# Attention and feed-forward in one kernel: other PSUM pools, one addition and one scaling moved, up to the first feed-forward

## The chip, the cores and the metric

The kernel runs on one core of one Trainium2 chip. The metric is the device time of one execution in microseconds (us). The engines are TensorE (PE, with its weight loads as PEld), VectorE (DVE), ScalarE (ACT), GpSimd (POOL), and SyncE (SP), which here issues every DMA.

## The reference

Inputs are q, k and v for 4 batches, 8 heads, 768 positions and head size 64, and two weights, 512x2048 and 2048x512, all float32 in value (the weights arrive as 64-bit words).

```
scores = q @ k.T / sqrt(64)
keep   = (key < n_sink) | (0 <= query - key < window)      # n_sink 4, window 128
a      = exp(scores - max);  a = a / (sum(a) + 1e-9)       # scores outside keep: -1e9
x      = (a @ v), heads side by side                       # 3072 rows of 512
h      = x @ w_in
g      = h if h >= 1, 0 if h <= -1, else (h + 1)^2 / 4
out    = g @ w_out
```

## The kernel before

The work on attention is cut into 64 units: one head and one half of the sequence (three blocks of 128 queries) of one batch. Eight units, one for each head, make a chunk, and a chunk of 384 finished rows goes through the feed-forward. The first 20 units (`NATIVE`) multiply in plain float32; each such product is a pair of records in the trace. Later units split the operands into two rounded parts. Attention of one chunk is interleaved with the feed-forward of the chunk before. Before the first feed-forward there is no such partner: the first ten units (0 to 9) run against the decoding of six weight blocks alone.

A native unit n goes through these steps:

- **S**: three products of q and k (L240), each into a PSUM bank of the pool `ps_a`. VectorE reads the bank, adds the mask and takes the row's extreme (L244); ScalarE takes the exponential and its sum (L247).
- **The scaling**: 1e-9 is added to the three sums on GpSimd (L252), VectorE takes the reciprocal (L253), and the three blocks of p are multiplied by it, on the engines that `NORM` names: block 0 (128 columns in the first half of a sequence) on VectorE (L267), blocks 1 and 2 (260 columns) on ScalarE (L265).
- **T**: two groups of transposes (L325, L327), each into a bank of `ps_a`, copied out by ScalarE (L328, L332).
- **V**: for two heads together, the product with v (L368) into a bank of `ps_a`, copied into `xn` by ScalarE (L370), then split in two parts by ScalarE and VectorE (L480, L481) as input of the feed-forward.

The feed-forward's first product (L440) writes the pool `ps_h` (2 banks), the second (L459) the pool `ps_o` (3 banks); `ps_a` has 3 banks. So until the first feed-forward five of the eight banks stand empty, and the three of `ps_a` go round among S, T and V. A bank is handed on when its last reader is done.

TensorE runs in the order in which the program is written: for each n, S of unit n, T of unit n-1, and, for odd n, V of units n-3 and n-2. The other engines' order is set by a scheduler with its own estimate of times, and each runs its list strictly in that order. SyncE's list holds, for each unit, the loads of q and k (two buffers: the load for unit n+2 waits for S of unit n), and behind them the loads of weight blocks. A weight block is numbered here w0, w1, ... in the order of use; it is decoded by four VectorE instructions (L151, L152, L153, L155) and a ScalarE cast (L154). Small tiles `vs_r` (44x64) for units after the 20th are loaded and cast early too (L296, L298).

Of the kernel before, what the change touches and what calls it, by code (L numbers as in the profile page):

```python
# [8 lines left out]
F32 = mybir.dt.float32  # L9
# [4 lines left out]
ALU = mybir.AluOpType  # L14

B, H, S, D = 4, 8, 768, 64
DM, DFF = 512, 2048
P = 128
NT = S // P
CT = 3  # L20
# [6 lines left out]
NATIVE = 20  # L27
# [1 line left out]

KL_POOL = range(20, 24)  # L30
GL_POOL = 0
NORM = "vaa"

CHECK = range(34, 34 + 2 * NJ)

# [15 lines left out]
def attn_ffn(ctx, tc, qk, vx, vs, par, w_in, w_out, out):  # L51
    nc = tc.nc
# [5 lines left out]
    ps_a = ctx.enter_context(tc.tile_pool(name="ps_a", bufs=3, space=bass.MemoryType.PSUM))  # L58
    ps_h = ctx.enter_context(tc.tile_pool(name="ps_h", bufs=2, space=bass.MemoryType.PSUM))
    ps_o = ctx.enter_context(tc.tile_pool(name="ps_o", bufs=3, space=bass.MemoryType.PSUM))  # L60
# [168 lines left out]
    def scores(u, i):  # L229
        b, h, t0 = u  # L230
        qs, k_s = st["qk", u]
        if i == 0:
            st["p", u] = [att.tile([P, CT, 260], F32, name="p"), att.tile([P, 2 * CT], F32, name="stat")]
        p, stat = st["p", u]
        t = t0 + i
        lo = KB if t == 0 else 0
        c0 = i * KB if t0 else max(0, (i - 1) * KB)
        ps = ps_a.tile([P, 512], F32, name="ps_a")
        for j, q in enumerate(qs):
            nc.tensor.matmul(ps[:, lo:260], lhsT=q[:, i * P:(i + 1) * P], rhs=k_s[:, c0:c0 + 260 - lo],  # L240
                             start=(j == 0), stop=(j == len(qs) - 1))
        peak_i = peak[:, units.index(u), i:i + 1]
        m = (m0, m1n if units.index(u) < NATIVE else m1, m2)[min(t, 2)]
        nc.vector.tensor_tensor_reduce(  # L244
            out=p[:, i, lo:260], in0=ps[:, lo:260], in1=m, scale=-0.0625 if units.index(u) < NATIVE else -0.125, scalar=3.0e38,
            op0=ALU.add, op1=ALU.min, accum_out=peak_i)
        nc.scalar.activation(p[:, i, lo:260], p[:, i, lo:260], AF.Exp, bias=peak_i, scale=-1.0,  # L247
                             accum_out=stat[:, i:i + 1])
        if i < CT - 1:
            return  # L250
        st.pop(("qk", u))
        nc.gpsimd.tensor_scalar(stat[:, CT:2 * CT], stat[:, 0:CT], 1.0e-9, None, op0=ALU.add)  # L252
        nc.vector.reciprocal(stat[:, CT:2 * CT], stat[:, CT:2 * CT])  # L253
        i0 = int(t0 == 0)
        c0 = 0
        if units.index(u) >= NATIVE:

            c0 = P
            nc.vector.tensor_tensor(p[:, i0:, KB:260], p[:, i0:, KB:260], p[:, i0:, 0:P], op=ALU.add)  # L259
        for i in range(CT):  # L260
            lo = KB if t0 + i == 0 else c0
            r = stat[:, CT + i:CT + i + 1]
            eng = NORM[i] if units.index(u) < NATIVE else "v"
            if eng == "a":
                nc.scalar.activation(p[:, i, lo:260], p[:, i, lo:260], AF.Copy, scale=r)  # L265
            else:
                (nc.gpsimd if eng == "p" else nc.vector).tensor_scalar(p[:, i, lo:260], p[:, i, lo:260], r, None,  # L267
                                                                       op0=ALU.mult)
        if units.index(u) < NATIVE:
            sk = None  # L270
        else:
            sk = att.tile([P, CT * NSINK], F32, name="sk")[:, :(CT - i0) * NSINK]
            nc.vector.tensor_copy(sk.rearrange("p (i s) -> p i s", s=NSINK), p[:, i0:, P:KB])
        st["p", u] = (p, sk)
# [78 lines left out]
    def av2(u):  # L353

        b, h, t0 = u
        T = CT * P
        pt = st.pop(("pt", u)).bitcast(F32).rearrange("p a i c q -> p a (i c q)")
        v_s = st.pop(("v", b, h // 2))
        st.pop(("sp", u))
        ps = ps_a.tile([P, 512], F32, name="ps_a")  # L360

        terms = [(2, 2 * CT - 1, 2 * CT)] + [(i, 2 * i + 1, 2 * i + 3) for i in range(CT - 1)] + [None]
        for n, t in enumerate(terms):
            for a in range(2):
                k, s0, s1 = t or (CT, 2 * CT - 1, 2 * CT)
                rhs = pt[:, a, s0 * P:s1 * P] if t else spn[(h + a) % 4]
                c = s0 // 2 * P
                nc.tensor.matmul(ps[a * D:a * D + D, c:c + (s1 - s0) * P], lhsT=v_s[:, k, a], rhs=rhs,  # L368
                                 start=(n == 0), stop=(n == len(terms) - 1))
        nc.scalar.copy(xn[:, h // 2, :], ps[:, :T])  # L370
# [41 lines left out]
    units = [(b, h, t0) for b, t0 in chunks for h in range(H)]  # L412

    def attn_steps(n):
        us = {k: units[n - k] for k in (-1, 0, 1, 2) if 0 <= n - k < len(units)}
        steps = []
        if n == 0:
            steps.append((0.0, lambda: load(us[0])))
        if -1 in us:
            steps.append((0.0, lambda: load(us[-1])))  # L420
        if 1 in us:
            steps.append((0.0, lambda: values(us[1])))
        qk = [(0.43 if n < NATIVE else 0.22, lambda i=i: scores(us[0], i)) for i in range(CT) if 0 in us]
        tp = [(0.43, lambda i=i: transp(us[1], i)) for i in range(2 if n - 1 < NATIVE else 1) if 1 in us]
        pv = [(1.0, lambda: av(us[2]))] if 2 in us else []
        if 2 in us and n - 2 < NATIVE:
            pv = [(1.6, lambda: av2(units[n - 3]))] if n % 2 else []
        steps += qk + tp + pv
        if n in CHECK:
            steps.append((0.0, lambda: recheck(n - CHECK[0])))  # L430
        return steps
# [125 lines left out]
    ps = ps_a.tile([P, 512], F32, name="ps_a")  # L557
# [124 lines left out]
```

## Time and profile before

| | us |
|---|---|
| time, median of 3 (lowest to highest) | 749.72 (746.22 to 750.14) |
| the profiled execution | 752.38 |
| its span, first to last instruction | 750.7 |
| TensorE busy / VectorE / ScalarE / GpSimd in the span | 703.2 / 509.2 / 500.3 / 277.4 |

Rows of windows give, for a stretch of the span, each engine's busy time and number of instructions, the clock granted to TensorE (1.00 is 2.4 GHz, 0.50 is 1.2 GHz), the DMA engines' mean busy share and GB/s. Rows of the chain give start, length and what the time went on, followed back from the end of the program. Rows of waits give engine, line, what released it, total us, times and the longest. Rows of a timeline give start, length, engine, line, operation, output<-input, sizes, and in brackets the idle time just before and what ended it. Rows of groups give count, busy us, mean ns of one, and the idle time before.

### The profile page before, as it was taken

The numbers are of one execution on the slowest core, as the hardware profiler recorded it, in microseconds if no ns is written. First come the engines' busy times: TensorE is split into PE (matmuls) and PEld (weight loads), VectorE is DVE, ScalarE is ACT, GpSimd is POOL, SyncE is SP. The second block draws the span as 40 slices with busy tenths as digits, with TensorE's granted clock in tenths as the row PEclk, the third lists the DMA queues.
The fourth block names the chain that finished last, engine by engine and source line by source line (L and its number), as shares of the span: only waits on it lengthen the run. The fifth ranks groups of instructions, "written<-read, shape, count | busy, mean of one in ns | idle before, by whom it ended". The sixth has DMA issues, their size and how long they took to land.

```text
span 750.7 us, 12243 instructions
## 1 busy us (share of the span) xinstructions
PE 703.2 (94%) x3857; PEld 618.4 (82%) x3857; DVE 509.2 (68%) x1360; ACT 500.3 (67%) x1307; POOL 277.4 (37%) x475
## 2 busy tenths in 40 slices
PE   5778899889999999999999999999989999999996
PEld 3447778778999999999888888898879888989985
DVE  8667885988655665578786886867777667842221
ACT  5787887757576665676676786777667676544342
POOL 3101123236346343245653645545565345410000
PEclk8889999989999999999999999999999999999999
DMA  8565674432131312233333433424333243001001
GB/s 252 174 184 179 213 238 145 124 91 62 42 97 44 99 51 69 92 103 108 113 106 100 130 117 100 122 79 146 121 91 114 90 122 122 9 1 43 0 1 46
DMA packets 49099, 77.73 MB, mean 104 GB/s; under 512 B 14980, under 2 KB 32900, under 8 KB 49028
## 3 DMA queue, kind: packets, MB, share of 16 engines
q1 hardware_dynamic: 49028, 76.89, 33.6%
q8 instruction: 32, 0.52, 0.3%
q14 instruction: 39, 0.32, 0.1%
HBM read 69.79 MB, written 7.08 MB: 102 GB/s over the span
## 4 chain that ended last, share of the span: by engine, by line
PE 46%; DVE 21%; DMA 12%; ACT 11%; POOL 4%; issue 4%; SPq 1%; ACTq 0%; POOLq 0%; DVEq 0%
PE o_ps L459 19%; PE h_ps L440 19%; DMA w<-w_in 3%; DMA again<-w_out 3%; PE ps_a L240 3%; DVE k_s L224 3%; ACT p L247 2%; DVE p L267 2%; PE ps_a L403 2%; DVE gl L451 2%; ACT k_s L222 2%; DVE g L449 2%; DVE o L152 2%; DVE p L259 1%; DMA again<-w_in 1%
## 5 line engine op out<-in xcount | busy, mean ns | idle before, releaser
L440 PE MATMUL h_ps<-x,wi 128*128 128x384 f32 x1536 | 312.3, 342 | 0.7 <-DVE x L481 0.7
L440 PEld LDWEIGHTS h_ps<-x,wi 128*128 128x128 f32 x1536 | 265.4, 189 | 10.5 <-DVE x L481 1.0
L459 PE MATMUL o_ps<-w,gh 128*128 128x512 f32 x768 | 245.4, 400 | 0.0
L459 PE MATMUL o_ps<-w,gl 128*128 128x512 f32 x384 | 151.4, 394 | 0.0
L459 PEld LDWEIGHTS o_ps<-w,gh 128*128 128x128 f32 x768 | 134.9, 189 | 15.9 <-issue 0.3
L247 ACT ACTIVATE p<-p,peak 128x260 f32<-128x260 f32 (+1 forms) x192 | 94.0, 490 | 40.1 <-DVE peak L244 39.3
L226 POOL TENSOR_TENSOR q_l<-r,q_h 128x384 fp32r<-128x384 f32 x44 | 45.1, 1025 | 199.0 <-ACT q_h L225 188.5
L449 DVE SCALAR_TENSOR_TENSOR g<-g,h_ps 128x384 f32<-128x384 f32 x128 | 70.1, 548 | 70.2 <-ACT g L448 69.5
L450 ACT CAST gh<-g 128x384 fp32r<-128x384 f32 x128 | 65.6, 512 | 76.2 <-DVE g L449 75.8
L447 ACT ACTIVATE g<-h_ps,half 128x384 f32<-128x384 f32 x128 | 73.8, 577 | 54.4 <-PE h_ps L440 53.3
L240 PE MATMUL ps_a<-k_s,q_h 128*128 128x260 f32 (+1 forms) x252 | 74.2, 348 | 23.1 <-DVE sk L342 11.6
L451 DVE TENSOR_TENSOR gl<-g,gh 128x384 fp32r<-128x384 f32 x112 | 69.3, 619 | 30.0 <-ACT gh L450 28.8
L459 PEld LDWEIGHTS o_ps<-w,gl 128*128 128x128 f32 x384 | 72.2, 188 | 17.7 <-DVE gl L451 0.3
L244 DVE CUSTOM_DVE_ANT_0 p<-ps_a,m 128x260 f32<-128x260 f32 (+1 forms) x172 | 66.0, 397 | 28.0 <-PE ps_a L240 27.1
L240 PEld LDWEIGHTS ps_a<-k_s,q_h 128*128 128x128 f32 x252 | 47.9, 204 | 38.2 <-issue 18.3
L224 DVE TENSOR_TENSOR k_s<-k_r,k_s 64x524 fp32r<-64x524 f32 (+1 forms) x40 | 43.0, 1075 | 37.7 <-ACT k_s L222 37.7
L448 ACT ACTIVATE g<-g 128x384 f32<-128x384 f32 x128 | 67.0, 523 | 2.5
L267 DVE TENSOR_SCALAR p<-p,stat 128x132 f32<-128x132 f32 (+1 forms) x152 | 57.6, 426 | 0.5
L252 POOL TENSOR_SCALAR stat<-stat 128x3 f32<-128x3 f32 x64 | 26.0, 406 | 84.2 <-ACT p L247 75.5
L347 POOL TENSOR_SCALAR_AFFINE_SELECT pt<-pt 128x384 fp32r<-128x384 f32 (+1 forms) x88 | 49.9, 567 | 18.1 <-DVE pt L340 14.7
L345 POOL TENSOR_SCALAR_AFFINE_SELECT pt<-pt 128x384 fp32r<-128x384 f32 (+1 forms) x88 | 49.3, 561 | 11.9 <-ACT pt L339 8.6
L403 PEld LDWEIGHTS ps_a<-pt,v_s 128*128 128x128 f32 x284 | 43.5, 189 | 1.8
(116 smaller groups left out, 916.9 us busy)
## 6 DMA issues: line engine op xcount, KB each, us to landing
r<-qk SPq DMA_DIRECT2D x44, 192.0 KB
k_r<-qk SPq DMA_DIRECT2D x32, 262.0 KB
w<-w_in SPq DMA_DIRECT2D x16, 512.0 KB
w<-w_out SPq DMA_DIRECT2D x16, 512.0 KB
again<-w_in SPq DMA_DIRECT2D x16, 512.0 KB
again<-w_out SPq DMA_DIRECT2D x16, 512.0 KB
out<-o SPq DMA_DIRECT2D x23, 256.0 KB
r<-vx SPq DMA_DIRECT2D x32, 128.0 KB
```

The lines of the kernel that those rows point to most:

```text
L224: eng.tensor_tensor(k_s[D:P], k_r[D:P], k_s[D:P].bitcast(F32), op=ALU.subtract)
L240: nc.tensor.matmul(ps[:, lo:260], lhsT=q[:, i * P:(i + 1) * P], rhs=k_s[:, c0:c0 + 260 - lo], start=(j == 0), stop=(j == len(qs) - 1))
L244: nc.vector.tensor_tensor_reduce(out=p[:, i, lo:260], in0=ps[:, lo:260], in1=m, scale=-0.0625 if units.index(u) < NATIVE else -0.125, scal ...
L247: nc.scalar.activation(p[:, i, lo:260], p[:, i, lo:260], AF.Exp, bias=peak_i, scale=-1.0, accum_out=stat[:, i:i + 1])
L267: (nc.gpsimd if eng == "p" else nc.vector).tensor_scalar(p[:, i, lo:260], p[:, i, lo:260], r, None, op0=ALU.mult)
L440: nc.tensor.matmul(h_ps[:, :T], lhsT=w_i[j][:, w, ct * P:(ct + 1) * P], rhs=x[:, y, ct], start=(ct == 0 and n == 0), stop=(ct == NCT - 1 a ...
L447: nc.scalar.activation(g, h_ps[:, :T], AF.Relu, bias=half, scale=0.5)
L448: nc.scalar.activation(g, g, AF.Square)
L449: nc.vector.scalar_tensor_tensor(g, g, 1.0, h_ps[:, :T], op0=ALU.min, op1=ALU.max)
L450: nc.scalar.copy(gh, g)
L451: (nc.gpsimd if row0 == GL_POOL else nc.vector).tensor_tensor(gl, g, gh.bitcast(F32), op=ALU.subtract)
L459: nc.tensor.matmul(o_ps[tt], lhsT=gg[:, tt * P:(tt + 1) * P], rhs=w_o[j][:, w], start=(j == js[0] and n == 0), stop=(j == js[-1] and n == 2))
```

## The change

Three things are changed for early units (the diff shows them in the order of the program: `NORM`, the bank of S, the addition, the choice of the scaling's engine, the bank of V). S of units 0 to 9 goes to `ps_o` and V of units 0 to 7 to `ps_h`; T stays in `ps_a`. The addition of 1e-9 of units 0 to 19 goes from GpSimd to VectorE, right ahead of the reciprocal in the program. For units 0 to 7 block 1 is scaled on VectorE, so that ScalarE has one of the three blocks in place of two; units 8 to 19 stay as they were.

```
-NORM = "vaa"
+NORM = "vva", "vaa"
...
-        ps = ps_a.tile([P, 512], F32, name="ps_a")
+
+        ps = ps_o.tile([P, DM], F32, name="o_ps") if units.index(u) < H + 2 else ps_a.tile([P, 512], F32, name="ps_a")
...
-        nc.gpsimd.tensor_scalar(stat[:, CT:2 * CT], stat[:, 0:CT], 1.0e-9, None, op0=ALU.add)
+        (nc.vector if units.index(u) < NATIVE else nc.gpsimd).tensor_scalar(
+            stat[:, CT:2 * CT], stat[:, 0:CT], 1.0e-9, None, op0=ALU.add)
...
-            eng = NORM[i] if units.index(u) < NATIVE else "v"
+            eng = NORM[units.index(u) >= H][i] if units.index(u) < NATIVE else "v"
...
-        ps = ps_a.tile([P, 512], F32, name="ps_a")
+        ps = ps_h.tile([P, 512], F32, name="h_ps") if units.index(u) < H else ps_a.tile([P, 512], F32, name="ps_a")
```

The scheduler makes a new order from it on every engine but TensorE. In the new program lines from 239 on stand one or two further down (L252 is L253, L253 is L255, L267 is L269, L298 is L300).

TensorE, from T of unit 4 to S of unit 6. Tile numbers in `ps_a` go round three banks. Before:

```order
L325 MATMUL ps_a_427<-ident_79,p_370 128x128 x2
L327 MATMUL ps_a_427<-ident_79,p_370 4x128
L325 MATMUL ps_a_434<-ident_79,p_370 128x128 x3
L368 MATMUL ps_a_448<-pt_335,v_s_311 64x128 x2
L240 MATMUL ps_a_466<-k_s_401,q_h_400 128x128
L240 MATMUL ps_a_470<-k_s_401,q_h_400 128x260
L240 MATMUL ps_a_474<-k_s_401,q_h_400 128x260
```

And now:

```order
L327 MATMUL ps_a_427<-ident_79,p_370 128x128 x2
L329 MATMUL ps_a_427<-ident_79,p_370 4x128
L327 MATMUL ps_a_434<-ident_79,p_370 128x128 x3
L370 MATMUL h_ps_448<-pt_335,v_s_311 64x128 x2
L241 MATMUL o_ps_466<-k_s_401,q_h_400 128x128
L241 MATMUL o_ps_470<-k_s_401,q_h_400 128x260
L241 MATMUL o_ps_474<-k_s_401,q_h_400 128x260
```

The order is the same. Before, the three products of S take over the banks of the two groups of T and of V, and wait for ScalarE's copies out of them; now they take over the banks of S of unit 5.

VectorE, where units 2 (p_268, stat_269) and 3 (p_315, stat_316) are scaled. Before:

```order
L253 RECIPROCAL stat_269<-stat_269 128x3
L152 SCALAR_TENSOR_TENSOR o_514<-w_287,o_514 128x512
L244 ISA p_315,peak_97<-ps_a_321,m1n_108 128x260
L244 ISA peak_97 128x1
L267 TENSOR_SCALAR p_268<-p_268,stat_269 128x128
L244 ISA p_315,peak_97<-ps_a_325,m2_106 128x260
L244 ISA peak_97 128x1
L153 SCALAR_TENSOR_TENSOR o_514<-w_287,o_514 128x512
L253 RECIPROCAL stat_316<-stat_316 128x3
L267 TENSOR_SCALAR p_315<-p_315,stat_316 128x128
```

And now:

```order
L253 TENSOR_SCALAR stat_269<-stat_269 128x3
L153 SCALAR_TENSOR_TENSOR o_514<-w_287,o_514 128x512
L255 RECIPROCAL stat_269<-stat_269 128x3
L253 TENSOR_SCALAR stat_316<-stat_316 128x3
L269 TENSOR_SCALAR p_268<-p_268,stat_269 128x128
L269 TENSOR_SCALAR p_268<-p_268,stat_269 128x260
L255 RECIPROCAL stat_316<-stat_316 128x3
L155 TENSOR_TENSOR wi2_153<-o_514,wi2_153 128x512
L269 TENSOR_SCALAR p_315<-p_315,stat_316 128x128
L269 TENSOR_SCALAR p_315<-p_315,stat_316 128x260
```

The masks of unit 3 now come ahead of everything of unit 2's scaling, and the addition for unit 3, which needs the last exponential of unit 3, stands ahead of both scalings of unit 2.

ScalarE in the same place. Before:

```order
L247 ACTIVATE p_268,stat_269<-p_268,peak_97 128x260
L298 CAST vsx0_137<-vs_r_1726 44x64
L247 ACTIVATE p_315,stat_316<-p_315,peak_97 128x128
L265 ACTIVATE p_268<-p_268,stat_269 128x260 x2
L247 ACTIVATE p_315,stat_316<-p_315,peak_97 128x260 x2
L328 COPY pt_335<-ps_a_334 128x2x128
L332 COPY spn2_145<-ps_a_334 4x128
L298 CAST vsx1_138<-vs_r_1871 44x64
```

And now:

```order
L300 CAST vsx0_137<-vs_r_1726 44x64
L330 COPY pt_251<-ps_a_302 128x3x128
L248 ACTIVATE p_268,stat_269<-p_268,peak_97 128x260
L248 ACTIVATE p_315,stat_316<-p_315,peak_97 128x128
L248 ACTIVATE p_315,stat_316<-p_315,peak_97 128x260
L300 CAST vsx1_138<-vs_r_1871 44x64
L248 ACTIVATE p_315,stat_316<-p_315,peak_97 128x260
L154 CAST wi2_153<-o_514 128x512
L267 ACTIVATE p_268<-p_268,stat_269 128x260
L267 ACTIVATE p_315<-p_315,stat_316 128x260
```

The casts of the two `vs_r` tiles now stand ahead of the last exponential of unit 2 and of unit 3, and all six exponentials of the two units ahead of the first scaling.

## Rows read from the trace of the kernel before

**Rows 1.** Windows: engines' busy us, clock, DMA share and GB/s by stretch.
```profile
4.70:57.10 52.40, 38.98 (x182) 24.87 (x182) 37.90 (x138) 39.14 (x125) 5.58 (x21) 0.80 0.69 213
22.00:28.80 6.80, 6.27 (x27) 4.24 (x28) 2.48 (x9) 5.33 (x18) 0.90 (x4) 0.50 0.40 122
28.80:49.60 20.80, 14.31 (x89) 9.06 (x88) 15.04 (x54) 17.68 (x57) 1.46 (x6) 0.99 0.66 195
49.60:56.10 6.50, 5.80 (x24) 3.67 (x25) 3.65 (x15) 5.63 (x18) 0.46 (x2) 0.50 0.45 133
57.10:120.00 62.90, 58.01 (x332) 48.00 (x331) 49.46 (x135) 48.39 (x141) 12.97 (x21) 0.97 0.64 205
```

**Rows 2.** Chain that ended last, 30 to 62 us: start, length, what.
```profile
30.09 4.25 DMA w<-w_in
...
36.69 0.36 ACT pt L328
...
39.72 1.48 PE ps_a L240 x6
...
42.07 5.26 DMA w<-w_in
...
49.09 0.16 ACT spn L332
...
49.29 2.55 PE ps_a L240 x6
...
53.09 4.60 DMA w<-w_out
```

**Rows 3.** Waits, 4.7 to 57.1 us: total, times, longest.
```profile
PE ps_a L325 <- ACT p L265: 7.5, 5, 2.1
PE ps_a L240 <- DMA q_h<-qk: 5.4, 2, 4.8
PE ps_a L240 <- DVE peak L244: 2.2, 6, 0.7
DVE stat L253 <- POOL stat L252: 2.1, 2, 1.4
PE ps_a L240 <- ACT xn L370: 1.0, 2, 0.8
PE ps_a L240 <- ACT pt L328: 0.7, 1, 0.7
PE ps_a L325 <- DVE peak L244: 0.6, 1, 0.6
PE ps_a L240 <- ACT spn L332: 0.5, 1, 0.5
```

**Rows 4.** Timeline of TensorE, 22 to 50 us.
```profile
22.53 0.88 PE L325 MATMUL ps_a<-ident,p 128*128 128x128 f32 x2 [2.10 <-ACT p L265]
...
30.56 1.37 PE L240 MATMUL ps_a<-k_s,q_h 128*128 128x128 f32 x6 [0.70 <-DVE peak L244]
...
33.33 0.73 PE L325 MATMUL ps_a<-ident,p 128*128 128x128 f32 x2 [1.40 <-ACT p L265]
...
49.29 2.53 PE L240 MATMUL ps_a<-k_s,q_h 128*128 128x128 f32 x6 [0.50 <-ACT spn L332]
```

**Rows 5.** Timeline of ScalarE, the two early casts.
```profile
21.44 0.24 ACT L298 CAST vsx<-vs_r 44x64 fp32r<-44x64 f32 x1 [1.32 <-DMA vs_r<-vs]
...
24.36 0.24 ACT L298 CAST vsx<-vs_r 44x64 fp32r<-44x64 f32 x1
```

**Rows 6.** Groups, 4.7 to 57.1 us: count | busy us, mean ns | idle before.
```profile
L247 ACT ACTIVATE p<-p,peak 128x260 f32<-128x260 f32 x20 | 10.1, 505 | 2.9 <-DVE peak L244 2.8
L265 ACT ACTIVATE p<-p,stat 128x260 f32<-128x260 f32 x20 | 9.1, 500 | 1.8 <-DVE stat L253 1.8
L253 DVE RECIPROCAL stat<-stat 128x3 f32<-128x3 f32 x10 | 1.7, 172 | 2.3 <-POOL stat L252 2.1
L104 DVE TENSOR_SCALAR m<-x,nw 128x260 f32<-128x260 f32 x1 | 0.4, 351 | 0.0
```

## The prediction

> **What bounds the kernel now.** I read the busy times by stretch first. After the first feed-forward product, at 57.1 us, TensorE is busy 58.0 of 62.9 us; in the stretch that the change touches, 4.7 to 57.1 us, it is busy 39.0 of 52.4, VectorE 37.9, ScalarE 39.1 [rows 1]. So no engine bounds the first 57 us: they wait for each other in turn, and what the change can give is time by which the feed-forward starts earlier. TensorE, nearly full from there on, would carry such a shift to the end.
>
> Next the chain of waits from 30 us on, which says which waits matter [rows 2]. It repeats: a weight block is loaded (4.25 us), its decoding holds VectorE and through it ScalarE, ScalarE's copy frees a bank of `ps_a` (the copies at 36.69 and 49.09 us), S of an odd unit can start (39.72 and 49.29 us), and only when it is done does SyncE reach the next weight load (42.07 and 53.09 us). The link "copy, then S" is a matter of banks alone.
>
> Last the waits of that stretch [rows 3]. TensorE stood 2.2 + 1.0 + 0.7 + 0.6 + 0.5 = 5.0 us for banks (ended by VectorE's read or ScalarE's copy of another tile), 7.5 us for the scaling of p ahead of T, and 5.4 us for q.
>
> **The change, part by part.**
>
> Banks. S no longer shares banks with T and V; in the new order its products follow V without a wait. All five bank groups of rows 3 go. Of their 5.0 us, 1.2 lie in the first 20 us, where two waits for q (5.4 us) end later anyway [rows 3], and I count these at nothing. The other seven waits run from 30.56 to 49.29 us, the first 0.70 and the last 0.50 us [rows 4], and make 3.8. I take -3.8; the ends are 0 (each is replaced by a wait for p) and -5.0.
>
> A page speaks for this: the Trainium skill, "Perfetto Trace Analysis", Matmul Optimizations, asks that all eight PSUM banks be used. By that rule alone all 5.0 us would come back, which is 744.7 us.
>
> Unit 2's scaling. This is the step that gets worse. Its T started at 22.53 us, after a stand of 2.10 us for ScalarE's scaling [rows 4], and from there to the end of S of unit 4 TensorE had almost no gap: it was busy 6.27 of 6.80 us [rows 1]. A later T is a later S of unit 4, one for one. In the new order VectorE does all masks of unit 3 and the addition for unit 3 ahead of both scalings of unit 2, and that addition needs the last exponential of unit 3. ScalarE has the second cast of a `vs_r` tile ahead of that. The first cast waited for its load until 21.44 us; the second ran at 24.36 us [rows 5], its load having landed at an unknown time before. If it runs no earlier than it did: it ends at 24.60, and an exponential of 0.505, the addition at the reciprocal's 0.172 and two scalings of at most 0.351 each (the only row of 260 columns with a scalar for each partition; one of the two has 128) [rows 6] give 25.98, +3.4 us. If its load is long there, the first cast ends at 21.68, a copy of 0.36 [rows 2], four exponentials (2.02) and the cast's 0.24 follow, and with the same 0.87 it is 25.17, +2.6. Both count each operation by its whole duration, and two of them have fewer columns, so I stay near the lower end: I take +2.7.
>
> Order of the exponentials. For units 4 to 7, too, the third exponential of the odd unit now stands ahead of the even unit's scaling on ScalarE: 0.505 us [rows 6] in two pairs, +1.0 (0 to +1.5, were the third pair on the path as well).
>
> One scaling fewer on ScalarE. It takes off 0.500 us a unit and puts 0.351 on VectorE beside it [rows 6]; T waits for the later one. At most 0.5 in each of three pairs, 1.5; I take -0.5, since VectorE has just finished masks there and is not free. Were VectorE late, it would be +0.35 a pair, +1.0.
>
> The addition. GpSimd's hop held VectorE 2.1 us in two waits, the longer 1.4 [rows 3]; that one is in unit 3's scaling, already counted. The other 0.7 goes: -0.7. On VectorE an addition of 128x3 costs about what the reciprocal of that size does, 0.172 [rows 6]; behind it queue the reciprocal and whatever masks and decoding follow, and TensorE's T waits for these. In units 8 to 19 VectorE is busy 49.5 of 62.9 us [rows 1], so twelve additions cost between 0 and 12 x 0.172 = 2.1; I take +0.3, as most fall into its free fifth.
>
> Sum: -3.8 + 2.7 + 1.0 - 0.5 - 0.7 + 0.3 = -1.0 us. The profiled execution took 752.38 us (span 750.7), so 751.4 in its frame; it was 2.66 above the median 749.72, so the forecast is **748.7 us**. All terms at their good ends but the second at +2.6, the hop's whole 2.1 gone: -5.0 + 2.6 + 0 - 1.5 - 2.1 + 0 = -6.0. At their bad ends, with half of the bank waits coming back: -1.9 + 3.4 + 1.5 + 1.0 + 0 + 2.1 = +6.1.
>
> **The rivals.** What this measurement can tell from no change is about 0.5%, 3.75 us.
>
> Faster, 744.6 us. TensorE's clock was at 1.2 GHz (0.50) from 22.0 to 28.8 and from 49.6 to 56.1 us, with 6.27 and 5.80 us of work in them [rows 1]. If work without bank waits keeps the clock at 2.4 GHz in the second stretch, half of 5.80, 2.9 us, comes back as well, and with the early 1.2 us of bank waits it is -1.0 - 2.9 - 1.2 = -5.1. For it: between the two stretches, with short waits, the clock was 0.99 [rows 1]. Against it: the waits for p (7.5 us, the largest group) stay and grow.
>
> Slower, 754.9 us. The same clock, the other way. Before, S of an odd unit came late, and the waits were many and short. Now S of both units is done early, and TensorE then stands in one piece until the even unit is scaled: up to six exponentials at 0.505 and a scaling at 0.500, 3.5 us, at T of units 4, 6 and 8. Before the fall at 22.0 it stood 2.10 us; a stand of 1.40 us at 33.33 brought no fall [rows 1, 4]. If it falls at two of these places, each costs half of about 6.2 us of work, 3.1, as in the row of 22.0 to 28.8 [rows 1]: -1.0 + 6.2 = +5.2. One fall more than before gives 751.8 and can't be told from no change; two decide.
>
> On this the Trainium skill, "TensorE: Matmul & The Clock Gate", A second HAM failure mode, describes a kernel that goes round PSUM banks and whose clock goes up and down for the short idles between its groups. That agrees with the clock of rows 1 and speaks against expecting a steady clock here; it would make the slower rival's 754.9.
>
> Hidden, 749.7 us. The gain up to S of unit 9 is met by the next weight load (53.09 us, 4.60 us) and by decoding two blocks, behind which the masks of unit 10 and the last split stand on VectorE, so the feed-forward starts when it did. For it: the chain goes through that load [rows 2]. Against it: SyncE issues that load when S of unit 9 is done, so it moves along. The Trainium skill, in the same page's HAM oscillation section, tells of a matmul kernel in which double-buffering PSUM gave no further gain; by that the time is this rival's.
>
> That the change doesn't do what it says, I hold for excluded but for 0.02: the order shows S in `ps_o`, V in `ps_h`, and the addition on VectorE.
>
> **How the numbers follow.** The forecast 0.37 (its own range 746 to 752, nearly all within 0.5%), hidden 0.10, faster 0.30, slower 0.21. Faster than 745.97: 0.30 and a little of the forecast's edge, 0.33. Slower than 753.47: 0.22. Within: 0.45. The range, 741.5 to 755, takes in both rivals' times and goes beyond the faster one, because the good ends of the terms and the kept clock can come together (-6.0 - 2.9).
>
> **What would show it.** In the trace after: no wait of L241 on TensorE for ScalarE's copies up to 57 us; T of unit 2 at 25 to 26 us; S of unit 9 ending near 50.5 in place of 51.8; the waits of T for p above 7.5 us in total; a first L442 within 2 us of 57.1. If T of unit 2 is no later than 23.5 us, the second term is wrong. If the clock shows one stretch at 0.50 or three, a rival holds.

## The result, and the profile after

The changed kernel takes 753.61 us (median of 7 runs, 751.13 to 756.08), the one before 749.57 beside it: ratio 1.0059, interval 1.0034 to 1.0085. It is slower by about 4.4 us, where 1.0 us of gain was forecast. The two profiled executions hide this: before is 752.38 us, above all seven of its runs here, after 752.61, near the bottom of its own. A profile is one execution here, and the executions of one kernel lie some 6 us apart, so each profile below is read for its mechanism and each time from the runs.

The windows of the changed kernel (columns as in [rows 1]):
```profile
4.70:57.10 52.40, 34.65 (x166) 23.97 (x168) 41.21 (x156) 35.86 (x116) 2.08 (x10) 0.87 0.68 212
22.00:30.00 8.00, 3.85 (x21) 2.67 (x22) 4.38 (x15) 4.67 (x16) 0.52 (x2) 0.57 0.30 104
30.00:50.00 20.00, 15.62 (x98) 10.99 (x96) 14.31 (x55) 15.41 (x52) 0.62 (x3) 0.91 0.63 189
50.00:61.00 11.00, 7.55 (x33) 4.76 (x33) 9.00 (x28) 7.64 (x25) 0.20 (x1) 0.69 0.55 174
57.10:120.00 62.90, 58.77 (x345) 48.05 (x342) 50.98 (x141) 48.30 (x140) 10.52 (x13) 0.97 0.63 206
```
In the first row TensorE is busy 4.3 us less than in [rows 1] and VectorE 3.3 us more; ScalarE lost 3.3 us, GpSimd 3.5. VectorE is now the busiest in a stretch in which none stood out. TensorE's mean clock there is 0.87, where it was 0.80.

The waits from 4.7 to 57.1 us:
```profile
PE ps_a L327 <- DVE stat L255: 9.1, 2, 5.3
...
PE o_ps L241 <- DMA q_h<-qk: 4.6, 1, 4.6
...
PE ps_a L327 <- ACT p L267: 4.3, 3, 3.1
...
DVE stat L253 <- ACT p L248: 3.1, 4, 1.8
PE ps_a L327 <- DVE p L269: 3.0, 2, 1.5
...
PE o_ps L241 <- DVE peak L245: 1.2, 4, 0.5
```
The waits for ScalarE's copies are gone, which is what the banks were to do; 1.2 us of waiting for VectorE's reads stays. But T (L327) now waits 9.1 + 4.3 + 3.0 = 16.4 us for p, against 7.5 in [rows 3], and for the reciprocal most of all. VectorE waits 3.1 us at the addition, in order, for exponentials.

TensorE's timeline at three places (T of unit 2, S of unit 9, T of unit 8 and the feed-forward's start):
```profile
26.15 0.66 PE L327 MATMUL ps_a<-ident,p 128*128 128x128 f32 x2 [5.30 <-DVE stat L255]
...
50.30 1.52 PE L241 MATMUL o_ps<-k_s,q_h 128*128 128x260 f32 x4 [0.20 <-DVE peak L245]
...
54.96 0.88 PE L327 MATMUL ps_a<-ident,p 128*128 128x128 f32 x2 [3.14 <-ACT p L267]
...
60.48 0.82 PE L442 MATMUL h_ps<-x,wi 128*128 128x384 f32 x2
```
T of unit 2 starts 3.6 us later than in [rows 4], and the first feed-forward product at 60.48 instead of 57.1 us.

ScalarE's timeline at units 2 and 3 shows the order behind the late T of unit 2, the casts of `vs_r` ahead of the third exponentials (compare [rows 5]):
```profile
21.57 0.24 ACT L300 CAST vsx<-vs_r 44x64 fp32r<-44x64 f32 x1 [1.67 <-DMA vs_r<-vs]
22.09 0.51 ACT L248 ACTIVATE p<-p,peak 128x260 f32<-128x260 f32 x1
...
24.60 0.24 ACT L300 CAST vsx<-vs_r 44x64 fp32r<-44x64 f32 x1 [1.02 <-DMA vs_r<-vs]
24.75 0.51 ACT L248 ACTIVATE p<-p,peak 128x260 f32<-128x260 f32 x1
```
And VectorE's timeline at unit 0 shows what an addition in VectorE's order means:
```profile
10.66 0.16 DVE L253 TENSOR_SCALAR stat<-stat 128x3 f32<-128x3 f32 x1
10.73 0.42 DVE L245 CUSTOM_DVE_ANT_0 p<-o_ps,m1n 128x260 f32<-128x260 f32 x1
...
11.43 0.69 DVE L153 SCALAR_TENSOR_TENSOR o<-w,o 128x512 int32<-128x512 int32 x1
12.03 0.68 DVE L152 SCALAR_TENSOR_TENSOR o<-w,o 128x512 int32<-128x512 int32 x1
12.63 0.17 DVE L255 RECIPROCAL stat<-stat 128x3 f32<-128x3 f32 x1
```
Two masks and two pieces of decoding stand between the addition and its reciprocal: 0.16 us of work ends 1.8 us ahead of the row that wants it.

### The profile page after: what moved, and what is told of

Same layout as the page of the kernel before. It is cut to its first block, busy times and chain, and to the rows that moved or that the text cites. A ratio compares the mean times of both kernels' runs of the same rounds, so it can differ in the third digit from the quotient of the medians.

```text
span 750.8 us, 12227 instructions
## 1 busy us (share of the span) xinstructions
PE 699.3 (93%) x3857; PEld 617.7 (82%) x3857; DVE 517.9 (69%) x1388; ACT 497.7 (66%) x1299; POOL 271.6 (36%) x455
## 4 chain that ended last, share of the span: by engine, by line
PE 42%; DVE 23%; DMA 13%; ACT 12%; POOL 4%; issue 4%; SPq 1%; POOLq 0%; ACTq 0%; DVEq 0%
PE o_ps L461 18%; PE h_ps L442 17%; ACT p L248 3%; DMA w<-w_out 3%; DVE k_s L224 3%; DMA again<-w_out 3%; DVE p L269 3%; DVE gl L453 2%; PE ps_a L405 2%; PE ps_a L241 2%; DMA again<-w_in 2%; DVE o L152 2%; DVE g L451 2%; DVE o L153 2%; ACT k_s L222 2%
## 5 line engine op out<-in xcount | busy, mean ns | idle before, releaser
L442 PE MATMUL h_ps<-x,wi 128*128 128x384 f32 x1536 | 310.9, 341 | 0.0
L442 PEld LDWEIGHTS h_ps<-x,wi 128*128 128x128 f32 x1536 | 264.4, 189 | 9.4 <-DVE g L451 0.5
L245 DVE CUSTOM_DVE_ANT_0 p<-ps_a,m 128x260 f32<-128x260 f32 (+1 forms) x152 | 58.9, 402 | 22.2 <-PE ps_a L241 21.3
L241 PE MATMUL ps_a<-k_s,q_h 128*128 128x260 f32 (+1 forms) x192 | 54.2, 310 | 13.6 <-DVE sk L344 11.9
L269 DVE TENSOR_SCALAR p<-p,stat 128x132 f32<-128x132 f32 (+2 forms) x160 | 60.2, 424 | 0.5
L241 PEld LDWEIGHTS ps_a<-k_s,q_h 128*128 128x128 f32 x192 | 35.8, 191 | 23.4 <-issue 17.4
L405 PE MATMUL ps_a<-pt,v_s 128*128 128x256 f32 (+1 forms) x284 | 44.0, 274 | 0.5 <-DVE peak L245 0.5
```

Of the source, the lines that this page charges most:

```text
L405: nc.tensor.matmul(z, lhsT=w, rhs=y, start=(n == 0), stop=(n == len(mms) - 1))
L442: nc.tensor.matmul(h_ps[:, :T], lhsT=w_i[j][:, w, ct * P:(ct + 1) * P], rhs=x[:, y, ct], start=(ct == 0 and n == 0), stop=(ct == NCT - 1 a ...
```

## The experiments

Each kernel was measured against the one before on the same chip in 5 rounds, with 6 to 12 executions of its own; a difference in us is (ratio - 1) x 749. Line numbers of edited kernels differ by up to three.

**Each edit alone.** Only the named hunks of the change are made.
```diff
# e1_banks: S in ps_o up to unit 9, V in ps_h up to unit 7
# e2_add:   (nc.vector if units.index(u) < NATIVE else nc.gpsimd).tensor_scalar(...)
# e3_norm:  NORM = "vva", "vaa"
```


> Only the banks are changed: scores of units 0 to 9 in ps_o, products with v of units 0 to 7 in ps_h; the addition stays on GpSimd and two blocks of three on ScalarE. Theory 1 (order): what costs the 4.0 us is the order that the scheduler makes of all three edits together (both casts of vs_r tiles and all six exponentials of two units ahead of the first scaling; T of unit 2 at 26.2 in place of 22.5 us). Here the casts stand behind the third exponential of each unit, so T of unit 2 starts at 22 to 23.5 us, the bank waits are gone, and the time is 1 to 4 us below before. Theory 2 (load): VectorE is the engine that bounds the first 26 us, and whatever is put on it costs; here nothing is put on it, so also 1 to 4 us below before. Theory 3 (banks): the banks themselves cost, because TensorE works in fewer, longer pieces and its clock falls in the stands between; then 2 to 4 us above before.

> Only the addition of 1e-9 of units 0 to 19 goes from GpSimd to VectorE. Order: the casts and exponentials stay as before, so within 1 us of before, T of unit 2 at 22 to 23 us. Load: 20 additions of about 0.1 to 0.17 us on VectorE, 1 to 3 us above before. Banks: no change.

> Only the scaling of block 1 of units 0 to 7 goes from ScalarE to VectorE. Order: the casts stay behind the third exponential of unit 2 and of unit 3, so within 1.5 us of before, T of unit 2 no later than 23.5 us. Load: 8 scalings of 0.35 us on VectorE, six of them before unit 6, 1.5 to 3 us above before. Banks: no change.

> The changed kernel once more, for a second profile and a time beside those of the three single edits. All theories: 752 to 755.5 us, ratio about 1.006; T of unit 2 at 25.5 to 26.5 us in this profile too, and TensorE standing 3 us ahead of T of unit 8 with a fall of its clock there.

Measured: banks 1.0027 (1.0003 to 1.0050), the addition 1.0075 (1.0052 to 1.0099), the scalings 1.0023 (1.0003 to 1.0044), all again 1.0062 (1.0043 to 1.0082). The addition by itself costs as much as the whole change. The banks alone gain nothing: they are 2.0 us above before (0.2 to 3.7), where Theory 1 and Theory 2 expected 1 to 4 us below and Theory 3 2 to 4 above. Their waits from 4.7 to 57.1 us show why no gain came:
```profile
PE ps_a L325 <- ACT p L265: 11.9, 5, 2.9
...
PE o_ps L240 <- DVE peak L244: 1.6, 4, 0.7
```
Of the 5.0 us of bank waits in [rows 3], the ones for copies are gone; the waits of T for p rose by 4.4 us, from 7.5 to 11.9. S came sooner and T waited for the same scaling.

**Where the addition's price lies.**
```diff
# e5_no_add: units 0 to 19
+ nc.vector.reciprocal(stat[:, CT:2 * CT], stat[:, 0:CT])        # no addition
# e6_add_early: nc.vector for units.index(u) < H; e7_add_late: for H <= units.index(u) < NATIVE
# e8_banks_norm: the change, with nc.gpsimd.tensor_scalar(...) as before
```


> The kernel before, but for units 0 to 19 the reciprocal on VectorE reads the sums themselves: the addition of 1e-9 is left out, on GpSimd and on VectorE. Theory 4 (the price of the third run is the addition's place in VectorE's queue: addition and reciprocal are two rows there, with pieces of the weights' decoding, up to 1.6 us of waiting for a weight among them, between the two or ahead of them): with no addition there is one row only and no hop to GpSimd, so TensorE's waits up to 165 us stay at or under the 27 us of the kernel before and the time is 0 to 2.5 us under it, ratio 0.997 to 1.000. Theory 5 (each new order of the rows costs some 2 us, whatever the edit, as the banks alone and the scalings alone did): ratio 1.002 to 1.004. Theory 3b (the clock: every edited kernel spent about 22 us at the half clock and the one before about 16): ratio 1.002, low stretches of about 22 us in most of its executions.

> The kernel before, with the addition on VectorE for units 0 to 7 only (their work stands in the first 45 us). Theory 4, by TensorE's waits in the third run (2.7 us more than before up to 60 us, 2.6 more from 60 to 165): about half of the third run's +5.6 us, ratio 1.003 to 1.005. If the whole price arises later, beside the feed-forward, where the profile of the third run first falls behind the one of before (0.8 us at 89 us, 5.8 at 121): ratio 1.000 to 1.002. If it all arises early: 1.006 to 1.008.

> The kernel before, with the addition on VectorE for units 8 to 19 only (their work stands from 45 us to 135 us). Theory 4: the other half of the third run's price, ratio 1.003 to 1.005, with waits of more than 2 us ahead of a transposition of unit 11 to 17. If the price arises late alone: 1.006 to 1.008. If early alone: 1.000 to 1.002.

> The changed kernel with the addition back on GpSimd: banks and scalings as changed. Theory 4 (the addition is the costly part): the bank waits are gone, and with the hop on GpSimd back the time is within 2 us of the kernel before, ratio 0.999 to 1.003. Theory 5 (every edit costs about 2 us, and together they saturate at 4 to 6): ratio 1.004 to 1.006, as with the addition. The prediction's own sum without the addition (banks -3.8, second unit's scaling +2.7, exponentials +1.0, scaling -0.5) gave -0.6 us, ratio 0.999.

Measured: without the addition 1.0002 (0.9988 to 1.0016); units 0 to 7 on VectorE 1.0065 (1.0042 to 1.0088); units 8 to 19 1.0025 (1.0007 to 1.0043); the change with the addition back on GpSimd 1.0006 (0.9988 to 1.0023). So the rest of the change costs nothing that the measurement can tell, and the addition takes it from 1.0006 to 1.0059 and 1.0062: 4.0 and 4.2 us. Most of its price comes from the first eight units, where Theory 4 had put half. Theory 5, that every new order costs 2 us, falls with the first and the last; the order of all three edits together (Theory 1) had fallen with the addition alone. With the addition back on GpSimd, T of unit 2 is on time again, in TensorE's timeline:
```profile
21.77 0.61 PE L325 MATMUL ps_a<-ident,p 128*128 128x128 f32 x2 [1.83 <-DVE p L267]
```

**ScalarE's casts, and units 0 and 1.**
```diff
# e9_all_cast_moved (the change) and e10_before_cast_moved (before)
- nc.scalar.copy(vs_s[0:44, i, :], vs_r)
+ (nc.gpsimd.tensor_copy if units.index(u) < NATIVE + 2 else nc.scalar.copy)(vs_s[0:44, i, :], vs_r)
# e11_add_units_0_1: before, nc.vector for units.index(u) < 2
# e12_all_but_units_0_1: the change, nc.vector for 2 <= units.index(u) < NATIVE
```


> The changed kernel with all its edits; the two casts of vs_r into vsx for units 20 and 21, which ScalarE makes early, are made on GpSimd. In the changed kernel they stand on ScalarE ahead of the third exponentials of units 2 and 3 and wait there for vs_r's transfers; in the run with the addition back on GpSimd the first stands behind unit 2's third exponential and the second behind unit 3's scalings, and the exponentials end 2 to 3 us sooner, at 19.6 and 21.6 us instead of 22 and 25. Theory 6 (these casts are the price): 2.5 to 4.5 us come back, ratio 1.000 to 1.002, third exponentials of units 2 and 3 done by 20 and 22.5 us. Theory 7 (the price is the addition and the reciprocal as two rows of VectorE, with decoding between them, at units 0 and 1): it stays, ratio 1.004 to 1.007.

> The kernel before with the same two casts on GpSimd. There they stand behind the third exponentials of units 2 and 3. Theory 6: they hold up less there, 0 to 1.5 us come off, ratio 0.998 to 1.000. If moving any row costs some 2 us: 1.002 to 1.004.

> The kernel before with the addition on VectorE for units 0 and 1 only. ScalarE's order is then the one of the run with units 0 to 7, whose casts of vs_r stand behind the third exponentials. Theory 7: the whole price of that run, ratio 1.005 to 1.008, since reciprocals of units 0 and 1 come 2.8 and 2.0 us behind their third exponential instead of 1.1 and 0.8. If each unit's addition costs alike: a quarter of it, 1.001 to 1.002. Theory 6 alone: no price here, 1.000 to 1.001.

> The changed kernel, with the addition on GpSimd for units 0 and 1 and on VectorE for 2 to 19. The casts of vs_r then stand as in the run with the addition back on GpSimd, behind unit 2's third exponential and behind unit 3's scalings. Theories 6 and 7 both: the price is gone but for that of the late units, ratio 1.000 to 1.003. If each unit's addition costs alike: 1.005.

Measured: 1.0079 (1.0049 to 1.0109), 1.0002 (0.9982 to 1.0022), 1.0026 (1.0003 to 1.0049), 1.0050 (1.0029 to 1.0070). Theory 6 falls, and in an instructive way. With the casts moved, ScalarE's third exponentials of units 2 and 3 did come sooner:
```profile
20.19 0.51 ACT L247 ACTIVATE p<-p,peak 128x260 f32<-128x260 f32 x1
...
22.20 0.51 ACT L247 ACTIVATE p<-p,peak 128x260 f32<-128x260 f32 x1 [0.42 <-DVE peak L244]
...
28.62 0.51 ACT L247 ACTIVATE p<-p,peak 128x260 f32<-128x260 f32 x1
```
They start 1.9 and 2.55 us ahead of the changed kernel's, and the third row, unit 4's third exponential, 4.3 us ahead of its counterpart there:
```profile
32.96 0.51 ACT L248 ACTIVATE p<-p,peak 128x260 f32<-128x260 f32 x1
```
The time is none the better: what looked like the whole loss, in the two profiles, is not what sets the end. Theory 7's claim for units 0 and 1 falls too: they carry 1.9 of the early units' 4.9 us, and taking them out of the change leaves 1.0050, which was expected if each unit's addition costs alike.

**The row, the chain, the clock.**
```diff
# e13_spare_row: before, and for units 0 to 7
+ nc.vector.tensor_scalar(spare, stat[:, 0:CT], 1.0e-9, None, op0=ALU.add)      # nobody reads spare
# e14_add_on_scalar: units 0 to 7
+ nc.scalar.activation(stat[:, CT:2 * CT], stat[:, 0:CT], AF.Copy, bias=1.0e-9)
# e15_all_without_add: the change, with e5's reciprocal
# e16_fill: before, ahead of each T of units 0 to 9, into a bank of ps_o
+ for _ in range(4): nc.tensor.transpose(idle[0][:, :P], ident, ident)
# e17_gpsimd_twice: before, behind GpSimd's addition of units 0 to 7
+ nc.gpsimd.tensor_scalar(stat[:, CT:2 * CT], stat[:, CT:2 * CT], 0.0, None, op0=ALU.add)
```


> The kernel before with one more row on VectorE for units 0 to 7: the sums plus 1e-9 go to a tile that nobody reads, while GpSimd's addition and the reciprocal stay as they are and in their places. Theory 8 (the price is the row itself: 0.16 us of VectorE and its wait for the third exponential in VectorE's order): like the run with the addition of units 0 to 7 on VectorE, ratio 1.004 to 1.008. Theory 7 (the price is the chain: exponential, addition, decoding in between, reciprocal, so that the reciprocal comes later): no price, 0.999 to 1.002.

> The kernel before with the addition of units 0 to 7 on ScalarE, which has just made the exponentials: no row more on VectorE, and the hop to GpSimd gone as well; ScalarE gets eight short rows more. Theory 7 (two rows of VectorE with others between): no price, ratio 0.998 to 1.002. Theory 8 (VectorE's row): no price either, as the row isn't VectorE's. If any engine on the way from scores to transposition pays for the row as VectorE does: 1.004 to 1.008.

> The changed kernel's banks and scalings, and no addition at all for units 0 to 19 (the reciprocal reads the sums). By the runs so far (no addition: 1.000; banks and scalings: 1.001) 0.998 to 1.002 under every theory but Theory 5 (each new order costs some 2 us), which gives 1.003 to 1.006. If it is below 0.998 it beats both kernels.

> The kernel before, with four more transpositions of the constant ident into a bank that nobody reads ahead of each unit's own, for units 0 to 9, so that TensorE stands less. Theory 3b (the half clock sets the time): fewer low stretches up to 57 us, mean clock of an execution 0.003 to 0.006 higher, ratio 0.996 to 0.999. If the clock hardly matters while TensorE waits for others: clock higher, ratio 0.999 to 1.003, the added rows falling into waits or just behind them.

> The kernel before with a second addition (of 0.0) on GpSimd behind the first, for units 0 to 7: the chain from the exponential to the reciprocal is longer by one GpSimd row (0.2 to 0.7 us each in the trace of before), and no row is added on ScalarE, VectorE or TensorE. Theory 7 (the later reciprocal is the price): ratio 1.003 to 1.007, reciprocals of units 0 to 7 later by about as much as with the addition on ScalarE or VectorE. Theory 8 (a row on an engine of the way from scores to transposition is the price): 0.999 to 1.002, GpSimd being idle there.

> The kernel before, unchanged, measured like the others: what a ratio of this study is worth. Expected 1.000 with an interval of about 0.002 to both sides; its profile shows what of the first profile of before (33.7 us at the half clock) is usual: by the mean clock of its executions, 0.990, some 15 us, and a span of 746 to 748 us instead of 750.7.

Measured: spare row 1.0027 (1.0011 to 1.0044), on ScalarE 1.0069 (1.0047 to 1.0090), the change without any addition 1.0025 (1.0009 to 1.0042), fillers 1.0071 (1.0046 to 1.0096), GpSimd twice 0.9987 (0.9973 to 1.0002), before against itself 1.0006 (0.9984 to 1.0029). The last says how to read the others: single ratios up to 1.0025 or so (banks, scalings, late units, units 0 and 1, the spare row, the change without any addition) stand at the edge of what means anything; 1.005 and above stand clear of it. But these six lie all above 1, from 1.0023 to 1.0027, with intervals that leave out 1.000. So it stays possible that many new orders cost some 2 us, though not each does. The change without any addition was expected at 0.998 to 1.002 under every theory but Theory 5; measured against its 1.0025, the addition's price inside the change is some 2.6 us and not 4.

The length of the chain alone is not the price. I add up, over units 0 to 7, the time from the end of the third exponential (with the read-out of its sum) to the end of the reciprocal, in one profile each:

| run | sum, us | ratio |
|---|---|---|
| no addition | 7.4 | 1.0002 |
| before itself | 8.8 | 1.0006 |
| VectorE, units 0 to 7 | 10.5 | 1.0065 |
| GpSimd twice | 14.3 | 0.9987 |
| ScalarE, units 0 to 7 | 18.1 | 1.0069 |

The profiles of the two costly runs in this table, VectorE's and ScalarE's, are each of the fastest of their six executions (749.96 and 751.23 us, medians 753.33 and 753.37), so they may show little of what is paid.

GpSimd's longer chain, read from its timeline at unit 0, and VectorE's reciprocal there:
```profile
11.22 0.67 POOL L252 TENSOR_SCALAR stat<-stat 128x3 f32<-128x3 f32 x1 [4.02 <-ACT p L247]
11.97 0.23 POOL L253 TENSOR_SCALAR stat<-stat 128x3 f32<-128x3 f32 x1
```
```profile
13.06 0.17 DVE L254 RECIPROCAL stat<-stat 128x3 f32<-128x3 f32 x1
```
This reciprocal ends 2.10 us behind its exponential, as late as where the addition is on ScalarE (2.10), and costs nothing. VectorE's own addition makes it 2.8 us in unit 0, which this run doesn't reach; for units 0 and 1 the two runs above speak. Theory 7 falls; Theory 8, that a row is paid for where its engine has the rest of the stage in its order, holds in its direction only: the spare row's 1.0027 lies below its 1.004 to 1.008, and ScalarE's row is paid for as well. The rows themselves, by groups, are small:
```profile
L253 ACT ACTIVATE stat<-stat 128x3 f32<-128x3 f32 x8 | 1.5, 193 | 0.0
```
```profile
L253 DVE TENSOR_SCALAR spare<-stat 128x3 f32<-128x3 f32 x8 | 1.4, 175 | 1.0 <-ACT p L248 1.0
```
Eight rows of 1.5 us cost 5.2 us of the time on ScalarE; eight of 1.4 us cost 2.0 as spare rows on VectorE, where addition and reciprocal stay as they were in the program.

Nor is a wait in VectorE's order the price by itself. In the run without the addition VectorE's reciprocals wait for the exponentials themselves, nearly as long as the changed kernel's additions (3.1 us), and that run costs nothing:
```profile
L253 DVE RECIPROCAL stat<-stat 128x3 f32<-128x3 f32 x10 | 1.7, 170 | 2.9 <-ACT p L247 2.9
```

The mean clock does not settle the price either. By the mean granted clock of all executions, the kernel before has 0.989 and the changed one 0.985, so it does lose clock; but the change with the addition on GpSimd has 0.986 and is as fast as before, and the fillers have 0.991, the highest of all, and are 5.3 us slower. Theory 3, the clock as the whole price, falls. A part of it is not excluded: over 132 executions of the kernel before, each taken against the mean of its own measurement, clock and time go together with a correlation of -0.55, about 1.5 us for 0.004 of clock, and over the 17 runs without fillers mean clock and ratio with -0.73.

The profiles show one place where clock and time go together. TensorE's order is the same in all kernels. Of the 20 profiles, 14 have a mean clock of 0.98 to 1.00 between the first feed-forward product and the 78th behind it (fillers not counted), and take 12.9 to 15.5 us from the one to the other; four have 0.90 and take 16.3 to 17.2 us; the addition alone has 0.83 and takes 20.5 us, the fillers 0.82 and 19.2 us. Here are the windows for GpSimd twice and for before itself:
```profile
58.25:71.89 13.64, 12.90 (x80) 10.91 (x79) 12.27 (x34) 11.44 (x34) 3.07 (x4) 1.00 0.67 208
```
```profile
54.41:71.54 17.13, 13.94 (x80) 12.19 (x79) 12.71 (x36) 11.75 (x34) 2.08 (x4) 0.90 0.61 186
```
Of the 3.5 us between them TensorE is busy for 1.0 and stands for 2.4, so a low clock and waiting come together here, and no run tells which brings the other. Both profiles of the kernel before have 0.90 there and the changed kernel's two 0.99 or more: it belongs to the spread of single executions and is not shown to be part of the change's price.

## Why the prediction was wrong

**Steps that held.** No S waited for a copy. T of unit 2 started at 26.15 us (forecast 25 to 26, so a little past it), by just the order that was read: the addition for unit 3 ahead of unit 2's scalings, a cast of `vs_r` ahead of the third exponential. The waits for p rose above 7.5 us. A scaling on VectorE took 0.350 us (forecast 0.351). Two signs failed: S of unit 9 did not come sooner (it ends at 51.8, forecast 50.5), and the first L442 was 3.3 us late, not within 2.

**The step that failed first: the banks, -3.8.** Its far end, 0, that each bank wait is replaced by a wait for p, is what happened: 4.4 us more waiting for p in the run with the banks alone. With the scalings, for which -0.5 was taken, and the exponentials' order, +1.0, the prediction's terms make -3.3 us; the run with banks and scalings measured +0.4 (-0.9 to +1.7). Unit 2's +2.7 is left out of these terms, because T of unit 2 is on time in that run.

**The step that was too small: the addition.** Its terms were unit 2's scaling +2.7, the hop -0.7 and twelve additions +0.3, together +2.3; it took about 4.1 us inside the change by the run with the addition back on GpSimd (2.6 by the one without any addition) and 5.6 alone. Three parts of the reasoning are answered. The hop on GpSimd, priced at -0.7, is worth nothing that can be measured: leaving the addition out gives 1.0002 (-0.9 to +1.2 us, which takes in the -0.7), and doubling it 0.9987. The later T of unit 2, right in the trace, is not where the price sits: with the casts moved it starts 2.7 us sooner, in TensorE's timeline,
```profile
23.43 0.41 PE L326 MATMUL ps_a<-ident,p 128*128 128x128 f32 x2 [2.93 <-DVE stat L252]
```
and the price stays. And the early additions, priced at only what waits in unit 2, carry most of it. So the miss divides into 3.7 us for the first step and 1.8 for the second: -1.0 + 3.7 + 1.8 = +4.5, measured +4.4. The sum closes by the way it is made, since both parts come from the same run; it is no proof of its own.

**The base under both.** The prediction let a shift of the feed-forward's start go through to the end one for one. The profiles speak against it. TensorE's first feed-forward product in the run with additions in units 0 to 7, and in the run with GpSimd twice:
```profile
53.61 0.87 PE L441 MATMUL h_ps<-x,wi 128*128 128x384 f32 x3
```
```profile
58.25 0.88 PE L441 MATMUL h_ps<-x,wi 128*128 128x384 f32 x3
```
4.6 us apart, and the spans are 748.2 and 748.1, each of one execution. Over the 19 profiles without fillers, that start and the span go together with a correlation of 0.29; the sum of TensorE's own waits from 4.7 to 165 us and the span with 0.79. Followed product by product, the correlation of the start with the span is 0.68 at about 65 us and 0.91 at about 175 us. So most of what sets the span of an execution happens between 57 and 175 us. The work of units 8 to 19 runs beside the feed-forward until about 165 us, and an early start can be spent there; the low clock behind the first feed-forward product, above, lies in that stretch too.

**The rivals.** "Slower, 754.9" came nearest in time, and its sign is there in part: a stand of 3.14 us at T of unit 8, one of its places, one of 5.30 at T of unit 2, which it did not name, and a low clock in three places of the windows after (0.57, 0.91, 0.69). But over the whole of 4.7 to 57.1 us the clock was higher than before, and clock lost before 57 us goes with the span by a correlation of 0.18 only over the 19 profiles; its cause is not shown. "Hidden" is right for the banks, with waits for p in the place of the weight load that it named. "Faster" priced the clock by the profile before, which was no usual execution: its mean clock was 0.978, where the kernel's executions have 0.989. In the second profile of the same kernel (before itself) the later low stretch is missing, with no change made:
```profile
49.60:56.10 6.50, 5.02 (x36) 3.86 (x36) 2.45 (x11) 5.29 (x17) 0.43 (x2) 1.00 0.78 241
```

**What stays open.** Why a row of 0.16 to 0.19 us costs about 0.6 us each in the first eight units when it is the real addition, and 0.25 as a spare row, isn't settled; the intervals (3.1 to 6.6 and 0.8 to 3.3 us) just touch. Removing GpSimd's hop and adding to it both leave the time alone, so I take it to be something of the busy engines' orders: the rows that move around it, since each edit also brings a new order and no run has the row without one. That is argued and not shown. A profile of one execution can't say in which unit it is paid. No kernel of these beat the one before by more than the measurement can tell.

The Trainium skill, "Perfetto Trace Analysis", Optimizing GPSIMD Operations, advises to prefer other engines to GPSIMD where possible, as it is generally slower. By this case's runs that advice does not pay for a tiny row in a stage where GpSimd stands idle: its row may take 0.67 us against VectorE's 0.16 and be free, while VectorE's costs.

## What to carry to other kernels

Price a row by what its engine's order holds, not by its length: here a short row on an idle, slower engine was free, and the same row on one of the engines that hand work to each other was not, though all of these were a quarter idle. A wait that a change removes is a gain only if nothing else ends just behind it: before counting bank waits, ask what the next instruction in that engine's order waits for. And test "the shift goes through to the end" on its own: look for the later stage where the engine still waits. Compare the profiled execution with the median of its kernel before reading a price, or the clock, from it.

## What the runs showed of the hardware

The same 128x3 addition took 0.16 us on VectorE, 0.19 on ScalarE and 0.23 to 0.86 on GpSimd. Thirty-six recorded filler products (5.9 us busy, 289 ns each) raised the mean clock of the executions from 0.989 to 0.991 and the time by 5.3 us, near their own busy time, though TensorE stood over 13 us in that stretch before. That they are paid one for one is not shown: in their profile the first feed-forward product starts at 53.32 us, the earliest of all, and what is lost comes behind it.
